# Banded attention followed by a gated MLP: dividing each pair's output instead of its attention weights, with one weight buffer fewer and a re-timed order

## The chip, the cores and the metric

The program runs on one core of one Trainium2 chip. The metric is the device time of one execution in microseconds (us), from a profiler-free run; a profiled execution has its own time as well. The engines are PE (TensorE, matrix products), DVE (VectorE), ACT (ScalarE), POOL (GpSimd) and SP (SyncE, which here only issues DMAs).

## The reference

Eight batches, eight heads, 576 tokens, head size 64, then a gated MLP on the 4608 joined tokens (512 to 1536 to 512), all in float32.

```python
scores = scale * np.matmul(q, k.transpose(0, 1, 3, 2))
thresh = np.max(scores, axis=-1, keepdims=True) - tau
scores = np.where(scores >= thresh, scores, -1000000000.0)
scores = scores - np.max(scores, axis=-1, keepdims=True)
attn = np.exp(scores)
attn = attn / (np.sum(attn, axis=-1, keepdims=True) + 1e-09)
attn_out = np.matmul(attn, v)
# x = attn_out as (tokens, 512)
out = (1 / (1 + np.exp(-(x @ w_gate))) * (x @ w_val)) @ w_out
```

Only scores within `tau` of a row's largest one keep a weight; the weights of a row are divided by their sum.

## The kernel before

**Attention.** The work is cut into 32 pairs (8 batches, 4 pairs of heads each; `b` and `hp` in the code, a name such as `0_3` is batch 0, pair 3). A pair has nine tiles of 128 query rows by 576 keys: four for each head and one, called `l`, that holds the 64 left-over rows of both heads. Per tile, in `tile_steps`: PE computes the scores `s` into PSUM (L638 in one plain float32 product for the first `NPS` pairs, L646 in split high and low halves for the others); DVE takes each row's maximum into `st` (L653); the threshold is made from it on POOL for early tiles and on DVE later (L662); ACT takes the exponential into `p` (L667); DVE zeroes what is under the threshold and adds up the row in the same instruction (L670, sums in `sm`). Then a group of two tiles (or the `l` tile) is normalised: DVE takes the reciprocal of the sums (L706) and POOL multiplies each tile of `p` by it (L708). PE transposes `p` (L719, and L732 for the last 64 keys), ACT copies the result out of PSUM into `pt` and `pl` (L677), and PE multiplies by the values (`av`, L755). ACT copies `av` into `xf`, the pair's output with 128 rows (2 heads of 64 columns) and 576 tokens. For batches 0 and 1 `xf` is split into halves for the MLP at once (`split_x`: ACT cast L765, POOL subtraction L767); for the others it goes to DRAM (`xp`, `xa`) and comes back later. The tokens of the left-over rows always go to DRAM.

**MLP.** Weights come from DRAM, are turned from raw words into high and low halves (`convert`: POOL L471, ACT L475, DVE L478 and L484, ACT L496, POOL L502), and are written back to DRAM. Batches 0, 1 and 2 are multiplied directly (`in_units` L815, `out_units` L858); the others in three double blocks with seven products instead of eight (`two_blocks`: `in_two` L1057, `out_two` L1122). The three direct blocks run on PE between the tiles of attention, from the moment that all four pairs of batch 0 are there; the double blocks follow.

**Order.** Nothing is ordered by hand. Every operation gets an engine, a cost and a key (its due time in tiles), and a list scheduler (`Plan.run`) with a model of buffers and DMA writes each engine's instruction order from them before the program runs; on the chip every engine then works strictly in that order and waits for semaphores. `SLOTS` gives the number of buffers of each kind, `LEAD` how many tiles ahead a pair's inputs are prepared, `CONV_IN` and `CONV_OUT` the due times of the weight conversions (first one, step), `AHEAD` how many units of matrix work ahead an MLP weight may be loaded, `SHIFT` by how many tiles everything from batch 1 on is due later, and `LAG` the delay that the scheduler assumes when an engine waits for another. MLP products have keys from 1e6 on, so that on PE they fill what attention leaves free. All DMAs but one are issued from SP's one queue, in order.

Of the kernel before, what the change touches and what calls it, by code (L numbers as in the profile page):

```python
# [43 lines left out]
class Plan:  # L44
# [10 lines left out]
    def buf(self, tag, shape, dtype, name, cls=None):  # L55
        return Buf(self, tag, shape, dtype, name, cls)
# [256 lines left out]
def kernel(  # L313
# [203 lines left out]
    class Visit:  # L517


        def __init__(self, b, hp, kind, first):  # L520
            self.b, self.hp, self.kind, self.first = b, hp, kind, first

            self.plain_s = 4 * b + hp < NPS
            self.of_tiles = {}
            self.name = f"{b}_{hp}{kind}"
            self.c0, self.c1 = {"": (0, SM), "a": (0, SM // 2), "b": (SM // 2, SM)}[kind]
            g0, g1 = [(0, (0, 1)), (1, (0, 1))], [(0, (2, 3)), (1, (2, 3))]
            left = [(None, (NJ,))]
            self.groups = {"": g0[:1] + left + g1[:1] + g0[1:] + g1[1:], "a": g0, "b": left + g1}[kind]
            self.with_left = kind != "a"  # L530
# [78 lines left out]
    def tile_steps(vis, g, i, key):  # L609

        h, qt = g.h, g.tiles[i]
        n = f"{g.name}{i}"


        s = buf("s", [P, 2, SM], F32, f"s{n}")
        kc = SL if i == 0 else 0
        sv = lambda: s.ap[:, :, :HALF]
        cols = None if h is None else slice(qt * P - vis.c0, (qt + 1) * P - vis.c0)
        if vis.plain_s:

            heads = [(0, SM, 0, SL), (1, SM, SL, P)] if h is None else [(h, qt * P, 0, P)]
            reads = [y for x, c0, *_ in heads for y in ((vis.q1, (x, int(c0 >= 2 * P))), vis.k1[x])]
        elif h is None:
            steps = [
                (lambda a=a: vis.q2.ap[:, a, vis.WM :], lambda c, z=z: vis.k2.ap[:, z, c])
                for a, z in ((0, 0), (0, 1), (1, 0))
            ]
            reads = [vis.q2, vis.k2]
        else:
            steps = [  # L630
                (lambda: vis.qd[h].ap[:, cols], lambda c, z=z: vis.kd[h].ap[:, z, c]) for z in range(2)
            ]
            reads = [vis.qd[h], vis.kd[h]]

        def plain_scores():
            for (x, c0, r0, r1), c in itertools.product(heads, range(2)):
                rows = slice(c * D, (c + 1) * D)
                nc.tensor.matmul(  # L638
                    s.ap[r0:r1, c, :HALF], vis.q1.ap[rows, x, c0 : c0 + r1 - r0],
                    vis.k1[x].ap[rows, kc : kc + HALF], start=True, stop=True, skip_group_check=True,  # L640
                )

        def scores():
            for m, (st, mv) in enumerate(steps):
                for c in range(2):
                    nc.tensor.matmul(  # L646
                        s.ap[:, c, :HALF], st(), mv(slice(kc + c * HALF, kc + (c + 1) * HALF)),
                        start=m == 0, stop=m == len(steps) - 1,
                    )
# [3 lines left out]
        op("DVE", 0.76, key, lambda: nc.vector.tensor_reduce(  # L653
            out=st.ap[:, 0:1], in_=sv(), axis=AX.XY, op=ALU.max, negate=True
        ), reads=[s], writes=[(st, 0)])
        thr = THR(vis.first)
        if thr == "ACT":
            op("ACT", 0.3, key, lambda: nc.scalar.activation(
                st.ap[:, 1:2], st.ap[:, 0:1], AF.Identity, bias=ntau_t[:, 0:1], scale=-1.0
            ), reads=[(st, 0)], writes=[(st, 1)])  # L660
        else:
            op(thr, 0.21 if thr == "DVE" else 0.3, key, lambda: {"DVE": nc.vector, "POOL": nc.gpsimd}[thr].tensor_scalar(  # L662
                out=st.ap[:, 1:2], in0=st.ap[:, 0:1], scalar1=-1.0, scalar2=ntau_t[:, 0:1],
                op0=ALU.mult, op1=ALU.add,
            ), reads=[(st, 0)], writes=[(st, 1)])
# [4 lines left out]
        op("DVE", 0.9, key, lambda: nc.vector.scalar_tensor_tensor(  # L670
            out=p(), in0=sv(), scalar=st.ap[:, 1:2], in1=p(),
            op0=ALU.is_ge, op1=ALU.mult, accum_out=g.sm.ap[:, i : i + 1],
        ), reads=[s, (st, 1)], writes=[(g.p, i), (g.sm, i)])
# [10 lines left out]
    class Group:  # L684


        def __init__(self, vis, h, tiles):
            self.vis, self.h, self.tiles = vis, h, tiles
            self.name = f"{vis.name}_{'l' if h is None else h}{tiles[0]}"
            n = self.n = len(tiles)  # L690
            c = "c" if h is None else ""
            self.p = buf("p" + c, [P, n * S], F32, f"p{self.name}")
            self.sm = buf("sm", [P, n], F32, f"sm{self.name}")

            self.z = h or 0
            if tiles not in vis.of_tiles:
                m = 1 if h is None else 2
                vis.of_tiles[tiles] = (
                    buf("pt" + c, [P, m, NJ, n * P], F32, f"pt{self.name}"),
                    buf("pl" + c, [P, m, P], F32, f"pl{self.name}"),  # L700
                )
            self.pt, self.pl = vis.of_tiles[tiles]

        def normalise(self, key):
            sm, p, n = self.sm, self.p, self.n
            op("DVE", 0.17, key, lambda: nc.vector.reciprocal(out=sm.ap, in_=sm.ap), writes=[sm])  # L706
            for i in range(n):
# [629 lines left out]
```

## Time and profile before

| | |
|---|---|
| time, three runs | 1343.53, 1349.85, 1351.82 us (median 1349.85) |
| profiled execution | 1344.67 us, of which the span of its instructions is 1342.9 us |
| granted TensorE clock | 0.999 |
| busy share of the span | PE 98%, weight loads 80%, DVE 71%, ACT 55%, POOL 48% |
| DMA | 311.55 MB in 138709 packets, mean 232 GB/s |

The span falls into three stretches. Until 96.79 us only attention and weight conversions run, since the first MLP product needs all of batch 0. From there to about 803 us PE alternates between attention and the direct MLP blocks. From 824.79 us on the double blocks run alone. A busy time is the union of the intervals in which an engine executed something; the idle time before an instruction is put down to what released it.

### The profile page before, as it was taken

How to read it: one execution, taken by the hardware profiler on the slowest of the kernel's cores; microseconds unless marked ns; L12 is line 12 of the kernel's file. 1: busy time of each engine (PE TensorE's matmuls, PEld its weight loads, DVE VectorE, ACT ScalarE, POOL GpSimd, SP SyncE). 2: the span in 40 equal slices, each digit the busy share in tenths (PEclk: the TensorE clock that was granted, in tenths of full speed). 3: DMA queues.
4: the chain of work that ended last, by engine and by line, in shares of the span. 5: the costliest groups of instructions: out<-in, count | busy, mean ns of one | idle time of the engine just before them, and what ended most of it. 6: DMA issues, size and time to landing. Idle time of an engine off the chain costs nothing.

```text
span 1342.9 us, 23617 instructions
## 1 busy us (share of the span) xinstructions
PE 1316.9 (98%) x8292; PEld 1078.1 (80%) x8292; DVE 952.0 (71%) x1918; ACT 732.9 (55%) x1349; POOL 639.6 (48%) x675
## 2 busy tenths in 40 slices
PE   7889999999999999999999999999999999999998
PEld 4568878888888888888888878888888888888887
DVE  7888777777777787777877853557955569554593
ACT  7787777767767677666767652213522235322242
POOL 7788968965867765767767641111001010001100
PEclk9999999999999999999999999999999999999999
DMA  8679889998878796897968848656685566756563
GB/s 302 178 230 340 273 249 295 280 265 214 269 207 263 226 276 178 239 288 239 260 209 239 253 147 321 203 184 207 208 294 190 194 198 209 244 180 205 185 220 119
DMA packets 138709, 311.55 MB, mean 232 GB/s; under 512 B 21856, under 2 KB 49760, under 8 KB 138592
## 3 DMA queue, kind: packets, MB, share of 16 engines
q1 hardware_dynamic: 138448, 310.04, 75.1%
q8 instruction: 67, 1.10, 0.3%
q14 instruction: 50, 0.41, 0.1%
q10 hardware_dynamic: 144, 0.00, 0.0%
HBM read 204.08 MB, written 54.53 MB: 193 GB/s over the span
## 4 chain that ended last, share of the span: by engine, by line
PE 88%; DMA 3%; POOL 2%; ACT 2%; DVE 1%; issue 1%; SPq 1%; POOLq 0%; DVEq 0%; ACTq 0%
PE m L815 14%; PE qb L1057 11%; PE av L755 10%; PE s L646 8%; PE tp L719 8%; PE qc L1057 7%; PE qa L1057 7%; PE o L858 6%; PE rb L1122 5%; PE rc L1122 4%; PE ra L1122 4%; PE s_l L646 2%; DMA wr<-in_moe_w_out_dram 1%; PE lk L732 1%; DMA wo<-wod 1%
## 5 line engine op out<-in xcount | busy, mean ns | idle before, releaser
L708 POOL TENSOR_SCALAR p<-p,zero_t,sm 128x576 f32<-128x576 f32 x256 | 216.3, 855 | 91.8 <-DVE sm L706 73.4
L653 DVE TENSOR_REDUCE st<-s 128x1 f32<-128x576 f32 x256 | 192.0, 753 | 82.1 <-PE s L646 75.5
L670 DVE SCALAR_TENSOR_TENSOR p<-s,st,p 128x576 f32<-128x576 f32 x256 | 205.6, 811 | 29.0 <-ACT p L667 20.9
L970 POOL TENSOR_TENSOR gA<-gA 128x512 f32<-128x512 f32 x18 | 24.1, 1340 | 422.7 <-DVE gA L1036 422.7
L667 ACT ACTIVATE p<-s,st 128x576 f32<-128x576 f32 x256 | 189.4, 748 | 48.5 <-DVE st L653 46.5
L677 ACT COPY pt<-tp 128x512 f32<-128x512 f32 x256 | 147.5, 587 | 55.8 <-PE tp L719 53.8
L646 PE MATMUL s<-kd,qd 128*128 128x288 f32 x896 | 161.3, 307 | 1.0 <-DVE p L670 0.7
L815 PE MATMUL m<-x,wi 128*128 128x512 f32 x576 | 161.1, 404 | 0.0
L719 PE MATMUL tp<-ident,p 128*128 128x128 f32 x1024 | 153.1, 276 | 8.0 <-POOL p L708 2.6
L719 PEld LDWEIGHTS tp<-ident,p 128*128 128x128 f32 x1024 | 118.9, 140 | 38.8 <-issue 9.3
L646 PEld LDWEIGHTS s<-kd,qd 128*128 128x128 f32 x896 | 132.7, 190 | 9.9 <-PE m L815 0.9
L755 PE MATMUL av<-pt,vs 128*64 128x256 f32 x1024 | 124.6, 385 | 0.8 <-ACT pt L677 0.7
L858 PE MATMUL o<-g,wo 128*128 128x512 f32 x432 | 117.8, 402 | 0.0
L815 PEld LDWEIGHTS m<-x,wi 128*128 128x128 f32 x576 | 99.3, 189 | 14.1 <-ACT pl L677 0.2
L1057 PE MATMUL qa<-xs_p,wa 128*128 128x512 f32 x432 | 109.6, 389 | 0.0
L994 DVE TENSOR_TENSOR qu<-qb,qp 128x512 f32<-128x512 f32 x72 | 49.8, 691 | 83.9 <-PE qb L1057 69.8
L755 PEld LDWEIGHTS av<-pt,vs 128*64 128x64 f32 x1024 | 67.8, 136 | 47.7 <-issue 10.3
L1057 PEld LDWEIGHTS qa<-xs_p,wa 128*128 128x128 f32 x432 | 81.1, 188 | 16.8
L858 PEld LDWEIGHTS o<-g,wo 128*128 128x128 f32 x432 | 75.3, 189 | 11.1 <-ACT pl L677 0.2
L815 PE MATMUL m<-x,ws 128*128 128x512 f32 x288 | 76.7, 406 | 1.2 <-ACT pl L677 0.8
L1032 ACT ACTIVATE gA<-qa 128x512 f32<-128x512 f32 x18 | 10.8, 598 | 103.3 <-PE qa L1057 103.3
L962 ACT CAST gs_p<-gA 128x512 fp32r<-128x512 f32 x54 | 32.4, 619 | 58.2 <-DVE gA L1036 25.1
(141 smaller groups left out, 2577.4 us busy)
## 6 DMA issues: line engine op xcount, KB each, us to landing
kd<-k SPq DMA_DIRECT2D x112, 320.0 KB, 5.8
wi<-wid SPq DMA_DIRECT2D x48, 512.0 KB, 6.9
wo<-wod SPq DMA_DIRECT2D x36, 512.0 KB, 7.0
wa<-wid SPq DMA_DIRECT2D x36, 512.0 KB, 4.3
ws<-sid SPq DMA_DIRECT2D x36, 512.0 KB, 4.9
wt<-sid SPq DMA_DIRECT2D x36, 512.0 KB, 4.8
wo_p<-sod SPq DMA_DIRECT2D x36, 512.0 KB, 4.9
qd<-q SPq DMA_DIRECT2D x112, 128.0 KB, 4.3
```

The source lines that it names most:

```text
L646: nc.tensor.matmul(s.ap[:, c, :HALF], st(), mv(slice(kc + c * HALF, kc + (c + 1) * HALF)), start=m == 0, stop=m == len(steps) - 1,)
L653: op("DVE", 0.76, key, lambda: nc.vector.tensor_reduce(out=st.ap[:, 0:1], in_=sv(), axis=AX.XY, op=ALU.max, negate=True), reads=[s], write ...
L667: op("ACT", 0.74, key, lambda: nc.scalar.activation(p(), sv(), AF.Exp, bias=st.ap[:, 0:1], scale=1.0), reads=[s, (st, 0)], writes=[(g.p, i)])
L670: op("DVE", 0.9, key, lambda: nc.vector.scalar_tensor_tensor(out=p(), in0=sv(), scalar=st.ap[:, 1:2], in1=p(), op0=ALU.is_ge, op1=ALU.mult ...
L677: return op("ACT", act(n), key, lambda: nc.scalar.copy(dst(), src.ap), reads=[src], writes=[part])
L708: op("POOL", 0.9, key, lambda i=i: nc.gpsimd.tensor_scalar(out=p.ap[:, i * S : (i + 1) * S], in0=p.ap[:, i * S : (i + 1) * S], scalar1=zer ...
L719: nc.tensor.matmul(tp.ap[:, c, :], self.p.ap[:, o + c * P : o + (c + 1) * P], ident, is_transpose=True, start=c == 0, stop=c == NJ - 1, sk ...
L755: nc.tensor.matmul(av.ap[h * D : (h + 1) * D, a:z], vis.vs.ap[:, j, h], m(h), start=i == 0, stop=i == len(ms) - 1, skip_group_check=True,)
L815: nc.tensor.matmul(m.ap, wv[:, a, c * P : (c + 1) * P], xs[c].ap[:, z, c0:c1], start=e == 0, stop=e == 11,)
L858: nc.tensor.matmul(acc.ap, wv[:, f, a], g[fg * ND + f].ap[:, z], start=(fg, f, a, z) == (0, 0, 0, 0), stop=(fg, f, a, z) == (NFG - 1, ND - ...
L1057: nc.tensor.matmul(acc.ap, wv[:, y, (2 * h + c) * P : (2 * h + c + 1) * P], xt[prod][c].get()[:, z], start=e == 0 and prod in FIRST, stop= ...
L1122: nc.tensor.matmul(acc.ap, w.ap[:, e, c, y], gt[prod][2 * g + c].get()[:, z], start=m == 0 and g == 0 and prod in FIRST, stop=m == 5 and g ...
```

## The change

For every pair but `0_3` (the last one of batch 0) the weights in `p` stay undivided: their reciprocal and the nine POOL multiplications go. In their place stands one step per pair, `late_normalise`. The nine sums of each row lie in one 128 x 32 tile (`sums`, three in rotation, filled with 1.0 at the start); DVE takes the reciprocals of nine columns and transposes the tile in blocks of 32 x 32 (`turned`); four DMAs write the nine rows of each block to a DRAM tensor `rd` (9 x 128); four DMAs read it back, each row broadcast to the 64 rows of its head, into `rb` (128 x 576); POOL multiplies `xf` by `rb`. Whatever reads `xf` now comes after that. `p` has three buffers instead of four, which makes room for `rb`. Plain scores are used for three pairs instead of four, and seven numbers of the scheduler change.

```diff
-    "p": 4, "pc": 1, "sm": 8, "st": 16, ... "xf": 2, "x": 6, "g": 12,
+    "p": 3, "pc": 1, "sm": 8, "st": 16, ... "xf": 2, "rb": 1, "x": 6, "g": 12,
-LEAD = 8
-CONV_IN, CONV_OUT = (36, 2), (56, 3)
+LEAD = 9
+CONV_IN, CONV_OUT = (36, 2.5), (56, 3)
-AHEAD = 4
+AHEAD = 5
-NPS = 4
+NPS = 3
-SHIFT = 35
+SHIFT = 50
-LAG = {"PE": 1.0, "DVE": 0.3, "ACT": 0.08, "POOL": 0.3, "SP": 0.08}
+LAG = {"PE": 0.8, "DVE": 0.2, "ACT": 0.3, "POOL": 0.3, "SP": 0.08}
+
+def LATE(b, hp):
+    return (b, hp) != (0, 3)
...
+    rows_of = [(lasting(f"sums{i}"), lasting(f"turned{i}")) for i in range(3)]
+    for sm, _ in rows_of:
+        nc.vector.memset(sm.t, 1.0)
...
-            op0=ALU.is_ge, op1=ALU.mult, accum_out=g.sm.ap[:, i : i + 1],
-        ), reads=[s, (st, 1)], writes=[(g.p, i), (g.sm, i)])
+            op0=ALU.is_ge, op1=ALU.mult, accum_out=g.sums(i),
+        ), reads=[s, (st, 1)], writes=[(g.p, i), g.parts[i]])
+
+    def late_normalise(vis, key):
+        n = 2 * NJ + 1
+        sm, rt, name = vis.sm, vis.rt, vis.name
+        op("DVE", 0.17, key, lambda: nc.vector.reciprocal(out=sm.ap[:, :n], in_=sm.ap[:, :n]), writes=[sm])
+        op("DVE", 0.2, key, lambda: nc.vector.transpose(out=rt.ap, in_=sm.ap), reads=[sm], writes=[rt])
+        rd = dram([n, P], f"rd{name}")
+        for c in range(P // 32):
+            rows = slice(32 * c, 32 * c + n)
+            op("SP", 0.1, key, lambda c=c, rows=rows: nc.sync.dma_start(
+                out=rd.t[:, 32 * c : 32 * c + 32], in_=rt.ap[rows]
+            ), reads=[rt], writes=[(rd, c)])
+        rb = buf("rb", [P, S], F32, f"rb{name}")
+        for h in range(2):
+            rows = slice(h * D, (h + 1) * D)
+            op("SP", 0.5, key, lambda h=h, rows=rows: nc.sync.dma_start(
+                out=rb.ap[rows, :SM],
+                in_=rd.t[h * NJ : (h + 1) * NJ].rearrange("t q -> (t q)").unsqueeze(0).to_broadcast([D, SM]),
+            ), reads=[rd], writes=[(rb, (h, 0))])
+            op("SP", 0.1, key, lambda h=h, rows=rows: nc.sync.dma_start(
+                out=rb.ap[rows, SM:], in_=rd.t[2 * NJ : n, h * SL : (h + 1) * SL].to_broadcast([D, SL])
+            ), reads=[rd], writes=[(rb, (h, 1))])
+        op("POOL", 1.5, key, lambda: nc.gpsimd.tensor_tensor(out=vis.xf.ap, in0=vis.xf.ap, in1=rb.ap, op=ALU.mult),
+           reads=[rb], writes=[vis.xf])
...
         def normalise(self, key):
+            if self.vis.late:
+                return
...
             if h == 1:
                 g.output(c, t - 1 + 0.3)
+        if vis.late:
+            late_normalise(vis, t)
```

Since the scheduler decides the order, the rows of the programs themselves show what moves. The first place is POOL's queue before the subtraction that completes `x_3`, the last input of the first MLP product. Before, eleven rows stand between the normalisation of pair `0_3`'s last group and `x_3`; these are the last seven of them and `x_3` (`ws`, `wa` are conversions, `k` is the split of a pair's keys, `p_0_00` belongs to batch 1):

```order
L662 TENSOR_SCALAR st_0_l_1188<-st_0_l_1188,ntau_t 128x1
L471 TENSOR_SCALAR wa_2_1241<-wr_2_1190,zero_t 128x512
L565 TENSOR_TENSOR k_1_1233<-kn_1_504,k_1_1233 128x640
L502 TENSOR_TENSOR ws_0_1250<-wa_0_881,ws_0_1250 128x512
L708 TENSOR_SCALAR p_0_00_1181<-p_0_00_1181,zero_t,sm_0_00_1210 128x576 x2
L471 TENSOR_SCALAR wa_0_1316<-wr_0_1246,zero_t 128x512
L502 TENSOR_TENSOR ws_1_1312<-wa_1_946,ws_1_1312 128x512
L767 TENSOR_TENSOR x_3_1327<-xf_3_1243,x_3_1327 128x512
```

Now, on the same engine from the same normalisation (L756, the pair that is still divided early) on:

```order
L756 TENSOR_SCALAR p_3_12_1190<-p_3_12_1190,zero_t,sm_3_12_1202 128x576 x2
L483 TENSOR_SCALAR wa_0_1281<-wr_0_1128,zero_t 128x512
L483 TENSOR_SCALAR wa_2_1288<-wr_2_1157,zero_t 128x512
L514 TENSOR_TENSOR ws_0_1286<-wa_0_857,ws_0_1286 128x512
L514 TENSOR_TENSOR ws_2_1382<-wa_2_915,ws_2_1382 128x4x128
L815 TENSOR_TENSOR x_3_1402<-xf_3_1304,x_3_1402 128x512
```

Four conversions are left between the two; the normalisation of batch 1's first tiles, a key split and the thresholds are gone from this stretch. The second place is PE's queue just before the first MLP product (`m_0_0_0`). Before (`tp`, `lk` are transposes, `s` scores, all of pair `1_0`):

```order
L755 MATMUL av_3_12_1271<-pl_3_l_1137,vs_3_570 64x64 x2
L719 MATMUL tp_0_000_1319<-ident,p_0_00_1181 128x128 x4
L719 MATMUL tp_0_001_1331<-ident,p_0_00_1181 128x128 x4
L646 MATMUL s_0_100_1340<-kd_0_1_839,qd_0_1_972 128x288 x4
L732 MATMUL lk_0_00_1355<-ident,p_0_00_1181 128x128
L815 MATMUL m_0_0_0_1373<-x_0_577,ws_0_465 128x512 x3
```

Now, from the same last value product of pair `0_3`:

```order
L803 MATMUL av_3_12_1349<-pl_3_l_1186,vs_3_567 64x64 x2
L661 MATMUL s_0_101_1387<-kd_0_1_1065,qd_0_1_1047 128x288 x4
L767 MATMUL tp_0_001_1397<-ident,p_0_00_1254 128x128 x4
L780 MATMUL lk_0_00_1405<-ident,p_0_00_1254 128x128
L767 MATMUL tp_0_l_1418<-ident,p_0_l_1296 128x128 x4
L780 MATMUL lk_0_l_1432<-ident,p_0_l_1296 128x128
L767 MATMUL tp_0_020_1441<-ident,p_0_02_1372 128x128 x4
L661 MATMUL s_0_120_1453<-kd_0_1_1065,qd_0_1_1047 128x288 x4
L767 MATMUL tp_0_021_1463<-ident,p_0_02_1372 128x128 x4
L780 MATMUL lk_0_02_1472<-ident,p_0_02_1372 128x128
L863 MATMUL m_0_0_0_1477<-x_0_604,ws_0_578 128x512 x3
```

Counted over the whole queue, PE has done two more score tiles and three more transposed tiles of pair `1_0` when the first MLP product comes. The third place is SP's queue at a late normalisation in the middle of the program (`sid` and `wi` are MLP weights on their way out and in, `qd` and `kd` the queries and keys of a coming pair):

```order
L841 DMA wi_3_0_4460<-wid_0_110 128x1024
L700 DMA rd_0_197<-turned_132 9x32 x4
L593 DMA qd_2_0_4573<-q_2_4567 64x512
L706 DMA rb_0_4576<-rd_0_197 64x512
L710 DMA rb_0_4576<-rd_0_197 64x64
L706 DMA rb_0_4576<-rd_0_197 64x512
L710 DMA rb_0_4576<-rd_0_197 64x64
L593 DMA qd_2_0_4573<-q_2_4567 64x512
L597 DMA kd_2_0_4607<-k_2_4541 64x2x640 x2
```

Eight DMAs are new there. The four reads of `rd` follow its four writes with one other DMA in between, and the inputs of the next pair stand behind them.

More of the change, by code (lines that the diff above doesn't have):

```diff
@@ L226 @@
     "kn": 1, "qn": 1, "vn": 1, "k2": 1, "q2": 1, "kd": 3, "qd": 3, "vs": 3,
-    "p": 4, "pc": 1, "sm": 8, "st": 16, "pt": 2, "pl": 2, "ptc": 1, "plc": 1, "xf": 2, "x": 6, "g": 12,
+    "p": 3, "pc": 1, "sm": 8, "st": 16, "pt": 2, "pl": 2, "ptc": 1, "plc": 1, "xf": 2, "rb": 1, "x": 6, "g": 12,
     "w": 9, "t2": 6,
 }
-LEAD = 8
-CONV_IN, CONV_OUT = (36, 2), (56, 3)
+LEAD = 9
+CONV_IN, CONV_OUT = (36, 2.5), (56, 3)
 EARLY = 16
-AHEAD = 4
+AHEAD = 5
 PAD = 64
-NPS = 4
+NPS = 3
 AV_COST = 0.0096
@@ L443, with lasting @@
     w_sb = {}
+    def lasting(name):
+        b = Buf(plan, None, [P, 32], F32, name)
+        b.t = cp.tile([P, 32], F32, tag=name, name=name)
+        return b
+    rows_of = [(lasting(f"sums{i}"), lasting(f"turned{i}")) for i in range(3)]
+    for sm, _ in rows_of:
+        nc.vector.memset(sm.t, 1.0)
     def convert(i, f, key):
@@ L523, in __init__ @@
             self.plain_s = 4 * b + hp < NPS
+            self.late = LATE(b, hp)
+            if self.late:
+                self.sm, self.rt = rows_of[(4 * b + hp) % len(rows_of)]
             self.of_tiles = {}
@@ L692, in __init__ @@
             self.p = buf("p" + c, [P, n * S], F32, f"p{self.name}")
-            self.sm = buf("sm", [P, n], F32, f"sm{self.name}")
+            if vis.late:
+                at = 2 * NJ if h is None else h * NJ + tiles[0]
+                self.sums, self.parts = (lambda i: vis.sm.ap[:, at + i : at + i + 1]), [(vis.sm, at + i) for i in range(n)]
+            else:
+                sm = self.sm = buf("sm", [P, n], F32, f"sm{self.name}")
+                self.sums, self.parts = (lambda i: sm.ap[:, i : i + 1]), [(sm, i) for i in range(n)]
             self.z = h or 0
@@ L1213, in attention @@
                 g.output(c, t - 1 + 0.3)
+        if vis.late:
+            late_normalise(vis, t)
         b, hp = vis.b, vis.hp
```

## Prediction

> **What bounds the kernel now.** I read the busy shares first, then busy time by stretch, then who waited for whom inside a stretch.
>
> ```profile
> PE 1316.9 (98%) x8292; PEld 1078.1 (80%) x8292; DVE 952.0 (71%) x1918; ACT 732.9 (55%) x1349; POOL 639.6 (48%) x675
> ...
> core 0: us, PE busy (x) PEld busy (x) DVE busy (x) ACT busy (x) POOL busy (x), PEclk, DMA share, GB/s
> 0.00:97.00 97.00, 80.62 (x648) 52.13 (x649) 78.58 (x169) 78.99 (x149) 75.43 (x115) 1.00 0.73 236
> 97.00:200.00 103.00, 100.11 (x636) 81.34 (x637) 82.15 (x170) 75.75 (x141) 83.21 (x86) 0.98 0.92 287
> 200.00:800.00 600.00, 597.14 (x4605) 498.78 (x4601) 457.59 (x1087) 412.90 (x776) 426.79 (x436) 1.00 0.84 243
> 800.00:1342.90 542.90, 539.03 (x2409) 445.87 (x2408) 333.66 (x495) 165.29 (x284) 54.21 (x40) 1.00 0.64 208
> ```
>
> PE is the bound: 26.0 us of 1342.9 are idle. 16.4 of the idle (97.00 - 80.62) lie before the first MLP product, 2.9 + 2.9 in the two stretches that follow, 3.9 at the end. No term of this change shortens PE's products by much, so all of the idle together, 1.9%, caps the gain. In the front, PE, DVE, ACT and POOL are each 78 to 83% busy: there the engines hand tiles to each other and no one is full.
>
> ```profile
> PE lk L732 <- ACT pt L677: 3.5, 5, 0.8
> PE s_l L638 <- DVE p L670: 2.0, 1, 2.0
> PE s L638 <- DVE p L670: 1.4, 2, 1.2
> ...
> DVE p L670 <- POOL st L662: 4.3, 6, 2.7
> DVE st L653 <- PE s L638: 3.6, 4, 2.0
> ...
> PE tp L719 <- POOL p L708: 2.2, 4, 0.9
> ```
>
> The first five rows are waits up to 97 us (in all, how many, the longest), the last one is PE's from 200 to 800 us. In the front DVE waits 4.3 us for a threshold that stands behind normalisations in POOL's queue, and PE then waits 3.4 for DVE. Later on PE waits for a normalisation itself for only 2.2 us in 600.
>
> **The change, part by part.** The removed work is large and mostly hidden.
>
> ```profile
> L708 POOL TENSOR_SCALAR p<-p,zero_t,sm 128x576 f32<-128x576 f32 x256 | 216.3, 855 | 91.8 <-DVE sm L706 73.4 <-PE s L646 9.2 <-PE av L755 4.0
> ...
> L565 POOL TENSOR_TENSOR k<-kn,k 128x640 fp32r<-128x640 f32 x2 | 3.1, 1559 | 0.3 <-PE av L755 0.3
> L767 POOL TENSOR_TENSOR x<-xf,x 128x512 fp32r<-128x512 f32 x4 | 5.1, 1270 | 0.3 <-ACT x L765 0.3
> L478 DVE SCALAR_TENSOR_TENSOR wb<-wb,wa 128x512 int32<-128x512 int32 x11 | 7.6, 691 | 3.4 <-ACT wb L475 3.4
> L706 DVE RECIPROCAL sm<-sm 128x2 f32<-128x2 f32 x17 | 2.8, 166 | 0.6
> L568 DVE SCALAR_TENSOR_TENSOR q<-qn,scale_t,q 128x640 fp32r<-128x640 f32 x2 | 2.2, 1114 | 0.0
> ```
>
> POOL loses 31 x 9 x 0.855 = 239 us and gains 31 products of 128x576, between the 1.27 of 512 columns and the 1.56 of 640, say 1.42: 44 us. It is busy 48% and not the bound, so of this only what waits for POOL counts.
>
> *Threshold.* Of the 4.3 us I take 3.3; 1.0 stays, as thresholds still stand behind conversions and the new product.
>
> *The last input of the MLP.*
>
> ```profile
> 80.97 0.17 DVE L706 RECIPROCAL sm<-sm 128x2 f32<-128x2 f32 x1
> ...
> 93.38 0.62 ACT L765 CAST x<-xf 128x512 fp32r<-128x512 f32 x1
> ...
> 91.07 1.63 POOL L708 TENSOR_SCALAR p<-p,zero_t,sm 128x576 f32<-128x576 f32 x2
> 92.68 1.41 POOL L471 TENSOR_SCALAR wa<-wr,zero_t 128x512 f32<-128x512 f32 x1
> 94.05 1.27 POOL L502 TENSOR_TENSOR ws<-wa,ws 128x512 fp32r<-128x512 f32 x1
> 95.29 1.26 POOL L767 TENSOR_TENSOR x<-xf,x 128x512 fp32r<-128x512 f32 x1
> ...
> 96.79 0.50 PE L815 MATMUL m<-x,ws 128*128 128x512 f32 x1 [0.75 <-ACT pl L677]
> ```
>
> The cast of `x_3` ended at 94.00, its subtraction began at 95.29 because POOL was full, and the first MLP product followed at 96.79. With four conversions left in that place POOL is free: 1.3 us.
>
> *DVE ahead of pair 0_3's last tile* (by the two programs' rows): one conversion more, two steps of 0.69; one more query split, 1.11; 7 reciprocals for 19, 12 x 0.166 = 2.0 saved; three block transposes, which the trace does not have, between the reciprocal's 0.17 and a query split's 1.11, taken at 0.2, as 32 columns are nearer to the reciprocal's 2 than to 640. Sum +1.1 us, with 1.0 to 3.8 by the ends.
>
> *PE work brought forward.*
>
> ```profile
> 108.62 0.69 PE L646 MATMUL s<-kd,qd 128*128 128x288 f32 x4
> 109.15 1.08 PE L815 MATMUL m<-x,ws 128*128 128x512 f32 x4
> ...
> 106.04 0.60 PE L719 MATMUL tp<-ident,p 128*128 128x128 f32 x4
> 106.39 0.71 PE L815 MATMUL m<-x,ws 128*128 128x512 f32 x2
> ```
>
> From start to next start a score tile takes 0.53 and a transposed tile 0.35. Two and three more of them before the first MLP product are 2.1 us of PE work done in idle time.
>
> *Later.* The 2.2 us that PE waited for `p` go; what was queued next on PE was already there, so nothing replaces them.
>
> *Pair 0_3 in split scores, `LEAD`, `CONV_IN`, three `p` buffers.* Counted at 0: PE executes four products of 288 columns per tile either way, the splits were prepared for other pairs beside attention before, and a `p` tile is held for less time. If that cover goes, a tile waits for one normalisation, 1.63 us, some three times in the front.
>
> *The way round through DRAM.* The first pair of rows is of the front, the second from 97 to 800 us.
>
> ```profile
> L1228 SPq DMA_DIRECT2D xp<-xf x3: 561/567/628, 36.4 to 76.0; - x3
> DMA to landing us min/median/max: 2.5/2.9/3.4
> ...
> L1228 SPq DMA_DIRECT2D xp<-xf x28: 522/611/1399, 98.6 to 782.8; - x28
> DMA to landing us min/median/max: 2.1/4.7/9.5
> ...
> SPq L578 <- ACT q L563: 126.0, 21, 10.8
> ...
> kd<-k SPq DMA_DIRECT2D x112, 320.0 KB, 5.8
> ...
> qd<-q SPq DMA_DIRECT2D x112, 128.0 KB, 4.3
> ...
> 802.90 22.05 PE L858 MATMUL o<-g,wo 128*128 128x512 f32 x96
> ...
> 810.58 1.29 POOL L970 TENSOR_TENSOR xb<-xb,xb 128x512 f32<-128x512 f32 x1 [15.59 <-DMA xb<-xp]
> ```
>
> The nearest DMA is the small one of 32 KB: 0.6 us to issue, landing after 2.9 us in the front and 4.7 (2.1 to 9.5) later. From the last sum to `rb`: 0.4 on DVE, four issues 2.4 of which the last lands 2.9 after its start, again 1.8 + 2.9: 9.8 us in the front, 13.4 later. SP waits in order, so behind the reads of `rd` stand the next pair's `qd` and `kd`; behind POOL's product stand thresholds and conversions. In the front, `xf` is complete some 12 us after the last sum (pair `0_3`: reciprocal at 80.97, cast of `x_3` at 93.38); without a reciprocal and two products of 0.82 between them it will be some 10, so `rb` is about in time. Later, a pair lasts (802.90 - 96.79) / 28 = 25.2 us. Eight DMAs per pair are those of the two rows for `kd` and `qd`; with `kn`, `qn`, `vs`, one or two from `xf` and some five of MLP weights SP issues an estimated 18, at 0.6 each 11 us. It gets 8 x 0.6 + 4.7 = 9.5 more: 20.5 of 25.2. It fits, and its 126 us of waiting for query splits (4.5 per pair) show the room. New waits on PE: between 0 and 28 us (rival below), taken at 1.5, near 0, as weights are asked for five units ahead. [...]
>
> *The end of attention.* After the last value product PE has 96 MLP products, 22.05 us, and the first double block's inputs are used 7.7 us after it. The new product delays `xf` by 1.42 or somewhat more, and by the new program's rows 70 products remain, 16.1 us: 9.1 of 16.1, hidden; a delay of over 7 us would show.
>
> The sum: -3.3 - 1.3 + 1.1 - 2.1 - 2.2 + 1.5 = -6.3 us, against the profiled 1344.67: 1338.4. That execution lay 5.2 under the median of the three runs; on their basis it is 1343.6. I say 1343.
>
> **The rivals.**
> *The front closes* (0.2). Every hand-over in it gets shorter by a reciprocal and a normalisation, and PE loses all waits but the start's: 16.4 less the 5 us before the first tile can be there, and 2.9 + 2.2 later: 1344.67 - 16.5 = 1328.2, 1333 on the runs' basis. For it: the waits of DVE and PE above feed each other. Against it: DVE's work ahead of the last tile does not fall.
> *Nothing* (0.2). ACT's casts of `x_0` to `x_2` and POOL's thresholds stand behind `rb`; three waits of 2 us cancel the -6.3: 1350.
> *SP becomes the bound, slower* (0.1). It decides from 25.2 us of SP per pair on: with the landing at its longest 9.5 in place of 4.7, SP has 25.3. Each us over costs 28. At 1 us over, 1338.4 + 28 = 1366, 1371 on the runs' basis. For it: the DMA share of 0.92 and 0.84 in these stretches and the order of the rows. Against it: SP's waits.
> *The clock* (0.05).
>
> ```profile
> 97.60:101.00 3.40, 3.40 (x10) 2.62 (x9) 3.29 (x8) 1.72 (x4) 0.49 (x3) 0.50 1.01 243
> ```
>
> Once, after gaps of 0.76 and 0.75, 3.4 us ran at a granted clock of 0.50, a loss of 1.7. A front with a different pattern has none or several: -1.7, or +1.7 for each; two more, 1347. [...]
>
> **How the numbers follow.** Forecast 0.45, its own range 1337 to 1350 (the DVE ends, the threshold from 0 to 4.3, run to run). The range must take in the front's closing at 1333 less a few us, and a part of the slower side: 1328 to 1360, which leaves out the SP case and the tails. A measurement of this kernel tells about 1% (13.5 us) from no change. Faster by over 1% (under 1336.4): most of the first rival, 0.15, and a little of the forecast: 0.19. Slower (over 1363.3): the SP case and a tail, 0.11. Within: 0.70.
>
> **What the changed profile would show.** The first MLP product at about 93 us, with PE idle before it down from 16.4 to about 11. The wait of DVE for `st` on POOL at 1 us; no wait of PE for a normalised `p` after 200 us. POOL's busy time near 445. SP's waits for `rd` near 28 x 4, without new waits of PE for `kd`, `wi` or `wo`. Such waits of over 5 us, casts of `x` that wait over 2 us for POOL, or a first product after 95 us, would make it wrong.

## The result, and the profile after

The changed kernel takes 1363.87 us (median of 6 runs) and the kernel before 1348.76 us (6 runs on the same chip). The ratio is 1.0119, 95% interval 1.0076 to 1.0162: **1.2% slower**, 16 us by the ratio and 15.1 by the medians. The forecast was 1343 us with a range to 1360. The profiled execution took 1364.27 us, 19.6 more than that of before: PE's idle time rose from 26.0 to 39.4 us, its busy time by 6.2.

The busy shares, the four stretches of before, and two groups of POOL, changed kernel:

```profile
PE 1323.1 (97%) x8290; PEld 1089.2 (80%) x8290; DVE 942.9 (69%) x1848; ACT 726.4 (53%) x1339; POOL 452.9 (33%) x419
...
0.00:97.00 97.00, 80.46 (x644) 55.59 (x645) 79.24 (x167) 77.16 (x145) 55.07 (x84) 0.98 0.83 261
97.00:200.00 103.00, 100.14 (x671) 82.07 (x670) 85.48 (x175) 79.97 (x153) 65.63 (x57) 0.97 0.98 304
200.00:800.00 600.00, 584.40 (x4426) 489.93 (x4426) 428.62 (x968) 388.19 (x731) 270.03 (x232) 0.99 0.85 249
...
L713 POOL TENSOR_TENSOR xf<-xf,rb 128x576 f32<-128x576 f32 x31 | 44.9, 1448 | 92.0 <-DMA rb<-rd 62.3 <-ACT p L682 11.5 <-DMA qd<-q 9.7
L957 POOL TENSOR_TENSOR s<-wi 128x512 f32<-128x512 f32 x24 | 33.0, 1376 | 106.8 <-DMA wi<-wid 101.9 <-DMA rd<-turned 4.4 <-POOL k L580 0.4
```

POOL is as light as forecast (445 us forecast, 452.9 measured; the product 1.45 us). But from 200 to 800 us PE is idle for 600 - 584.40 = 15.6 us, where it was 2.9 before. L957 is the first addition of the weight sums that the double blocks need (L909 before). POOL waited 20.8 us for its load in the kernel before, and waits 101.9 now; ACT's cast of the sums (L920 before, L968 now) waited 0.4 us for POOL, and now 18.6. Kernel before, 97 to 800 us:

```profile
POOL s L909 <- DMA wi<-wid: 20.8, 9, 4.3
...
ACT s L920 <- POOL s L909: 0.4, 1, 0.4
```

Waits between 97 and 800 us in the changed kernel (total, times, longest), for PE, ACT, POOL and SP's queue:

```profile
PE lk L780 <- ACT pt L718: 4.5, 1, 4.5
PE s L661 <- DVE p L685: 3.7, 4, 3.1
PE tp_l L767 <- ACT pt L718: 3.6, 3, 1.9
PE tp L767 <- ACT xf L718: 3.1, 2, 2.6
...
ACT s L968 <- POOL s L957: 18.6, 10, 3.6
...
POOL s L957 <- DMA wi<-wid: 101.9, 20, 9.6
POOL xf L713 <- DMA rb<-rd: 48.1, 11, 14.8
...
SPq L706 <- DMA rd<-turned: 50.0, 25, 4.5
...
SPq L593 <- ACT q L578: 7.9, 4, 3.2
```

PE's loss is not spread out: five stalls of over 1 us between 200 and 800 us (at 354.58, 390.07, 423.94, 518.90 and 683.47 us) make 13.5 of the 15.6. The chain of waits of the changed kernel shows the third of them from its start at SP:

```profile
404.47 0.62 SPq L597
...
405.14 2.01 SPq L841
...
407.26 1.03 SPq L1267
...
408.34 0.65 SPq L1278
...
409.72 6.12 DMA wi<-wid
...
415.97 1.29 POOL s L957
...
422.80 0.61 ACT s L968
423.41 0.49 ACT pt L718
...
423.94 0.33 PE tp_l L767
```

The load of a weight for the sums goes out behind a row of other issues and lands 6.1 us after its own; POOL, whose next work this is, is already waiting; ACT's cast of the sum (L968) waits for POOL; the tile copy `pt` stands behind that cast in ACT's fixed order; PE waits 1.95 us for the copy. The stall at 390.07 has this form too. The load takes no longer than it did: from its issue to its last semaphore update in the trace, `wi` took 6.9 us in the kernel before and 6.8 now (medians of 48). What moved is when it is issued and when POOL asks for it.

The largest stall (4.54 us at 518.90) has the same form with ACT's cast of an `x` that came back from DRAM (`xa`, landing 6.27 us after its issue) in place of the sum. Here SP's queue shows how a wait for `rd` reaches a load; SP's wait from 490 to 512 us and two of its issues:

```profile
SPq L706 <- DMA rd<-turned: 4.1, 1, 4.1
...
496.05 0.48 SPq L706 DMA_DIRECT2D rb<-rd  x1
...
511.45 0.43 SPq L1301 DMA_DIRECT2D xa<-xa  x1
```

SP stands 4.1 us for `rd`, then issues eighteen DMAs with hardly a gap, and only then comes the load of `x`. The stalls at 354.58 and 683.47 us start at the round trip itself (`rd` landing 4.99 and 5.67 us after its issue, `rb` 2.79 and 2.68, then POOL's product, a sum, ACT's cast, ACT's exponential).

PE also runs at half clock more often: twice before its first MLP product, and behind the stalls of 4.54 and 3.08 us. These are the stretches of the changed kernel (granted clock is the third number from the end):

```profile
44.20:47.60 3.40, 3.40 (x18) 1.92 (x18) 2.99 (x8) 2.01 (x3) 0.84 (x3) 0.50 0.77 311
102.20:109.00 6.80, 6.34 (x21) 4.82 (x20) 5.98 (x13) 4.74 (x9) 3.05 (x3) 0.50 1.05 321
518.60:522.00 3.40, 3.09 (x9) 2.42 (x10) 0.59 (x1) 3.40 (x8) 3.07 (x3) 0.50 0.09 23
682.50:689.30 6.80, 5.83 (x20) 5.05 (x21) 4.04 (x10) 3.60 (x8) 3.25 (x3) 0.50 1.03 282
```

Together 20.4 us at 0.50 against 3.4 before. Half of the difference, 8.5 us, is an estimate of what that added to the profiled execution. The two stretches behind the stalls alone cost 5.1 us by the same estimate.

### The profile page after: what moved, and what is told of

Read it like the earlier page. It is cut to its first block, busy times and chain, and to the rows that moved or that the text cites. A ratio compares the mean times of both kernels' runs of the same rounds, so it can differ in the third digit from the quotient of the medians.

```text
span 1362.5 us, 23334 instructions
## 1 busy us (share of the span) xinstructions
PE 1323.1 (97%) x8290; PEld 1089.2 (80%) x8290; DVE 942.9 (69%) x1848; ACT 726.4 (53%) x1339; POOL 452.9 (33%) x419
## 4 chain that ended last, share of the span: by engine, by line
PE 80%; DMA 9%; SPq 4%; ACT 2%; DVE 2%; issue 2%; POOL 2%; POOLq 0%; ACTq 0%; DVEq 0%
PE m L863 11%; PE qb L1105 11%; PE av L803 8%; PE qa L1105 7%; PE qc L1105 7%; PE s L661 7%; PE o L906 6%; PE tp L767 6%; PE rb L1170 5%; PE rc L1170 4%; PE ra L1170 4%; DMA rd<-turned 1%; PE s_l L661 1%; DMA xp<-xf 1%; DMA kd<-k 1%
## 5 line engine op out<-in xcount | busy, mean ns | idle before, releaser
L661 PE MATMUL s<-kd,qd 128*128 128x288 f32 x928 | 169.4, 306 | 5.1 <-DVE p L685 4.3
L863 PE MATMUL m<-x,wi 128*128 128x512 f32 x576 | 165.5, 409 | 1.4 <-ACT pt L718 1.4
L767 PE MATMUL tp<-ident,p 128*128 128x128 f32 x1024 | 157.4, 278 | 7.0 <-ACT xf L718 3.8
L661 PEld LDWEIGHTS s<-kd,qd 128*128 128x128 f32 x928 | 141.6, 190 | 20.0 <-DVE p L685 5.7
L767 PEld LDWEIGHTS tp<-ident,p 128*128 128x128 f32 x1024 | 122.1, 142 | 31.3 <-issue 6.4
L863 PE MATMUL m<-x,ws 128*128 128x512 f32 x288 | 80.4, 412 | 0.6 <-ACT pt L718 0.5
L713 POOL TENSOR_TENSOR xf<-xf,rb 128x576 f32<-128x576 f32 x31 | 44.9, 1448 | 92.0 <-DMA rb<-rd 62.3
L957 POOL TENSOR_TENSOR s<-wi 128x512 f32<-128x512 f32 x24 | 33.0, 1376 | 106.8 <-DMA wi<-wid 101.9
```

The source lines that it names most:

```text
L661: nc.tensor.matmul(s.ap[:, c, :HALF], st(), mv(slice(kc + c * HALF, kc + (c + 1) * HALF)), start=m == 0, stop=m == len(steps) - 1,)
L767: nc.tensor.matmul(tp.ap[:, c, :], self.p.ap[:, o + c * P : o + (c + 1) * P], ident, is_transpose=True, start=c == 0, stop=c == NJ - 1, sk ...
L863: nc.tensor.matmul(m.ap, wv[:, a, c * P : (c + 1) * P], xs[c].ap[:, z, c0:c1], start=e == 0, stop=e == 11,)
```

## The experiments

Each group of runs has its own runs of the kernel before (medians 1348.9 to 1350.3 us), so ratios are compared; "us" behind a ratio is the ratio's distance from 1 times 1350. On this scale the changed kernel is +16.1. PE's idle time is that from 200 to 800 us in the profile (2.9 before, 15.6 after).

**Is it the round trip?** The eight DMAs are planned, but not issued; the order stays. The four reads are edited as the writes are.

```diff
-            op("SP", 0.1, key, lambda c=c, rows=rows: nc.sync.dma_start(
-                out=rd.t[:, 32 * c : 32 * c + 32], in_=rt.ap[rows]
-            ), reads=[rt], writes=[(rd, c)])
+            op("SP", 0.1, key, lambda: None, reads=[rt], writes=[(rd, c)])
...
-        op("POOL", 1.5, key, lambda: nc.gpsimd.tensor_tensor(out=vis.xf.ap, in0=vis.xf.ap, in1=rb.ap, op=ALU.mult),
+        op("POOL", 1.5, key, lambda: nc.gpsimd.tensor_tensor(out=vis.xf.ap, in0=vis.xf.ap, in1=ones, op=ALU.mult),
```

> The changed kernel with the same order on every engine, but the eight DMAs per pair that carry the reciprocal sums (`rd`, `rb`) are not issued, and POOL multiplies `xf` by a constant tile of ones; the transport of the sums is left out. Theory 1 (POOL, freed of normalisations, runs the weight sums as soon as their loads land, the loads land later than planned, and ACT's casts of the sums, in ACT's fixed order, hold up tile copies and exponentials that PE waits for): PE's stalls at 354 and 683 us, which the chain of waits leads back to `rb`, go; those at 390, 424 and 519, led back to late weight loads, stay at least in part: 1352 to 1359 us. Theory 2 (the round trip itself: eight more DMAs per pair on SP's queue and the waits for `rd` make every load late): all five go and the time is that of before or better, 1342 to 1349. Theory 3 (the new numbers of the order, not the round trip): no change, 1362 to 1366.

Measured 1338.55 us, ratio 0.9925 (0.9909 to 0.9942), -10 us. All stalls are gone:

```profile
200.00:800.00 600.00, 598.75 (x4586) 503.56 (x4586) 444.37 (x1004) 402.05 (x752) 275.85 (x235) 1.00 0.81 241
```

So the transport costs 26 us, and what is left of the change gains 10. Theory 1 in its first form falls: the stalls that led to late weight loads went too. POOL is as light here, and still waits 54.4 us for the loads of the sums between 97 and 800 us, but no stall of PE follows.

**What of the round trip?** Three kernels keep all eight DMAs and the order, and take waits away by changing what is read: POOL's product reads ones (`e5`), the fills of `rb` read a constant tensor in DRAM (`e6`), or both (`e7`). The first edit is that of `e5`, the second, made in the narrow reads too, that of `e6`. All three leave the sums out of the result. The product that reads ones takes 1.17 us in place of 1.45.

```diff
-in0=vis.xf.ap, in1=rb.ap, op=ALU.mult
+in0=vis.xf.ap, in1=ones[:, :1].to_broadcast([P, S]), op=ALU.mult
```

```diff
-in_=rd.t[h * NJ : (h + 1) * NJ].rearrange("t q -> (t q)").unsqueeze(0).to_broadcast([D, SM]),
+in_=fixed[h * NJ : (h + 1) * NJ].rearrange("t q -> (t q)").unsqueeze(0).to_broadcast([D, SM]),
```

> The changed kernel with the same order; all eight DMAs per pair are issued and SP still waits for the landing of `rd`, but POOL's product reads a constant of ones and does not wait for `rb` (the sums reach no output). If the loss of 25 us that leaving out the transport showed comes from POOL's wait for `rb` and what stands behind it on POOL and ACT: near 1339 to 1344 us. If it comes from SP (its issue time and its wait for `rd` hold up the loads behind) or from the bytes: 1357 to 1366.

> The changed kernel with the same order and the same eight DMAs per pair, but the four that fill `rb` read a constant tensor in DRAM instead of `rd`, so SP waits for no landing of `rd` (about 50 us of waiting between 97 and 800 us); POOL still waits for `rb`. The sums reach no output. If SP's wait in order is the cause: most of the 25 us go, 1339 to 1347. If it is SP's issue time (8 x 0.6 us per pair) or the traffic: 1356 to 1366. If it is POOL's wait for `rb`: in between, since `rb` lands some 5 us earlier.

> Both of the edits before together: the eight DMAs per pair are issued and move their bytes, but nobody waits for them. What is left above the run without transport (1339 us) is the price of SP's issue time and of the traffic alone: 1339 to 1343 if the waits are the cause, 1356 to 1366 if issue time or traffic is.

In a fourth kernel, on top of `e7`, each read fills one row of `rb`:

```diff
-out=rb.ap[rows, :SM],
-in_=fixed[h * NJ : (h + 1) * NJ].rearrange("t q -> (t q)").unsqueeze(0).to_broadcast([D, SM]),
+out=rb.ap[h * D : h * D + 1, :SM],
+in_=fixed[h * NJ : (h + 1) * NJ].rearrange("t q -> (t q)").unsqueeze(0),
```

> The kernel of the run in which all eight DMAs are issued and nobody waits for them (1348 us), but each of the four reads fills one row of `rb` in place of 64: SP issues as many, 10 MB fewer are moved. Without any transport it was 1339. If the traffic is what those 9 us are: 1338 to 1342. If SP's issue time is: 1346 to 1350.

| run | SP waits for `rd` | POOL waits for `rb` | bytes of `rb` | ratio (interval) | us | PE idle |
|---|---|---|---|---|---|---|
| changed kernel | yes | yes | all | 1.0119 (1.0076 to 1.0162) | +16.1 | 15.6 |
| `e5` | yes | no | all | 1.0090 (1.0056 to 1.0125) | +12.2 | 12.3 |
| `e6` | no | yes | all | 0.9993 (0.9972 to 1.0013) | -0.9 | 7.3 |
| `e7` | no | no | all | 0.9993 (0.9971 to 1.0015) | -0.9 | 6.6 |
| `e9` | no | no | 1/64 | 0.9929 (0.9910 to 0.9948) | -9.6 | 3.0 |
| `e1` | none issued | | | 0.9925 (0.9909 to 0.9942) | -10.1 | 1.3 |

The last column from the rows of 200 to 800 us, of `e5`, `e6`, `e7` and `e9` in this order:

```profile
200.00:800.00 600.00, 587.75 (x4479) 494.30 (x4478) 432.44 (x982) 393.10 (x738) 264.64 (x234) 0.99 0.85 250
```
```profile
200.00:800.00 600.00, 592.73 (x4529) 498.38 (x4527) 439.96 (x997) 398.43 (x749) 274.48 (x237) 1.00 0.87 252
```
```profile
200.00:800.00 600.00, 593.38 (x4522) 499.20 (x4521) 440.79 (x994) 397.82 (x747) 267.25 (x236) 1.00 0.87 253
```
```profile
200.00:800.00 600.00, 597.04 (x4567) 502.24 (x4567) 443.51 (x1004) 401.43 (x752) 270.87 (x237) 1.00 0.83 242
```

`e5` and `e7` differ in what the reads of `rb` read, and so in SP's wait for the landing of `rd` (50.0 us in `e5`, none in `e7`): 13 us by the ratios, give or take 6. The other source is not the reason: the wide reads landed 3.0 us after their issue from `rd` in `e5` and 3.4 from the constant in `e7` (medians). The largest stall goes with this wait; PE's waits for a tile copy before `lk`, in `e5` and in `e7`, from 97 to 800 us:

```profile
PE lk L784 <- ACT pt L722: 4.7, 2, 4.4
```
```profile
PE lk L784 <- ACT pt L722: 0.8, 1, 0.8
```

`e6` and `e7` differ in POOL's wait for `rb` (37.9 us in `e6`, none in `e7`): nothing by the ratios, as long as `rb` is filled early. With SP's wait in place, POOL's adds about 4 (changed kernel against `e5`), which is not clear of noise, as the intervals overlap. `e7` and `e9` differ by 8.7 us, give or take 4, through the width of the reads; that is not the bytes alone, as the issue of such a read got shorter too, from `e7` to `e9` (ns, shortest, median, longest):

```profile
L710 SPq DMA_DIRECT2D rb<-fixed x54: 444/594/1163, 124.1 to 786.0; - x54
```
```profile
L710 SPq DMA_DIRECT2D rb<-fixed x55: 214/253/1376, 120.5 to 799.5; - x55
```

Bytes and issue time of these reads are not told apart. The four writes of `rd` and the four one-row reads that `e9` keeps cost nothing that shows (0.5 us against `e1`, within the intervals).

**Is it ACT's cast of the sums?** The casts of L968 keep their length and wait for nothing.

```diff
-            op("ACT", act(512), key, lambda t=t: nc.scalar.copy(full(t, 0), f32(full(t, 1))), writes=[t])
+            op("ACT", act(512), key, lambda: nc.scalar.copy(free, f32(free)), writes=[t])
```

> The changed kernel with the same order, but ACT's casts of the weight sums (L968) read and write a tile that is always ready, so they keep their 0.6 us and wait for nothing; the rounded upper part of the sums is left out. Theory 1: the stalls of PE that run through that cast (354, 390, 424, 553, 683 us) go with the half clock behind them, the one of 519 us (a cast of x that waits for its load) stays: 1348 to 1353 us. Theory 2 (loads late for PE by themselves): the stalls come back through another instruction, 1358 to 1366. Theory 3: 1362 to 1366.

1361.6 us, ratio 1.0097 (1.0080 to 1.0115). It gains at most a few us: the stalls at 354, 390, 424 and 683 us are gone, but that at 519 has grown from 4.54 to 6.30, and there are new ones of 1.64 at 440, 2.21 at 480 and 2.42 at 799 us. So the cast carries stalls, but is not their cause: loads that are late reach PE by another instruction.

**Is it the numbers?** `e3` and `e16` are the kernel before with the new numbers (with three and four tiles of `p`), `e4` the changed kernel with the old ones, `e17` the same without transport, `e20` late normalisation in the first three pairs alone, with the old numbers. Of the diff of the change, `e3` and `e16` take the numbers from `LEAD` to `LAG` (`e3` also `"p": 3`), the other three undo them (and keep `"p": 3`). `e20` has in addition:

```diff
-    return (b, hp) != (0, 3)
+    return b == 0 and hp != 3
```

> The kernel before with only the new numbers: three tiles of `p`, LEAD 9, CONV_IN 2.5, AHEAD 5, NPS 3, SHIFT 50 and the new LAG; normalisation as before. Theories 1 and 2: the numbers alone cost little, 1343 to 1354 us. Theory 3: the loss is there without the late normalisation, 1358 to 1368.

> The changed kernel with the old numbers (LEAD 8, CONV_IN 2, AHEAD 4, NPS 4, SHIFT 35, the old LAG), keeping the late normalisation, three tiles of `p` and one of `rb`. Theories 1 and 2: casts of sums on ACT still wait for POOL and loads, the stalls come at other places, 1354 to 1372 us. Theory 3: the loss goes, 1342 to 1350.

> The kernel before with the new numbers LEAD, CONV_IN, AHEAD, NPS, SHIFT and LAG, but its four tiles of `p`; normalisation as before. With three tiles it took 1360.6 us. If the missing tile is what cost 11 us there (normalised tiles are held longer): 1346 to 1353. If the other numbers did: 1357 to 1364.

> The changed kernel with the old numbers and without the transport (constant ones in place of `rb`; the sums are left out). With the new numbers it took 1339 us. If the gain of 11 us against the kernel before is that of the freed POOL: 1336 to 1342. If the new numbers are needed for it, as the changed kernel with old numbers at 1380 suggests: 1345 to 1356.

> The changed kernel with the old numbers, three tiles of `p`, and the late normalisation only in the first three pairs of batch 0; all other pairs normalise their tiles as the kernel before does. If the loss is made between 200 and 800 us by 28 round trips: 1343 to 1356, near the kernel before. If the round trip or the missing tile of `p` already costs in the front: 1357 to 1368.

| normalisation | old numbers | new numbers |
|---|---|---|
| of `p`, as before | 0 | +8.9 (`e3`, 1.0034 to 1.0099), +10.1 with four `p` (`e16`, 1.0057 to 1.0094) |
| late, with transport | +30.4 (`e4`, 1.0193 to 1.0257) | +16.1 |
| late, no transport | -6.1 (`e17`, 0.9940 to 0.9970) | -10.1 |
| late in three pairs of the front | +4.3 (`e20`, 1.0017 to 1.0047) | |

The numbers are worth nothing by themselves: 9 to 10 us lost with the old normalisation (the missing tile of `p` is not why), 4 gained without transport, 14 gained with it. With the transport they take off some of its loss. With both sets of numbers the transport is what costs: 36.5 us with the old ones, 26.2 with the new. `e20` shows no gain of the late normalisation in the front, with its transport there and three tiles of `p`.

**Ways round the wait.** All keep the whole computation. `e8` lets the planner place the reads and the product later; `e14` and `e15` keep the order and let four or eight other DMAs of SP go ahead of the reads; `e11` issues the reads from POOL, `e18` from ACT with the landing planned in; `e12` has three DMAs per pair in place of eight, `e13` the same with the reads on POOL.

The edits of `e8`, of `e14` (`LATER` holds the four reads, `FLUSH` POOL's products; `e15` has 8), of `e18` and of `e12`; `e11` and `e13` only put `nc.gpsimd` for `nc.sync` at the reads, of the changed kernel and of `e12`.

```diff
-            ), reads=[rd], writes=[(rb, (h, 0))])
+            ), reads=[rd], writes=[(rb, (h, 0))], lag=3.0)
...
-           reads=[rb], writes=[vis.xf])
+           reads=[rb], writes=[vis.xf], lag=2.5)
```

```diff
         for o in order:
+            if o.emit in LATER:
+                held.append(o)
+                left = 4
+                continue
+            if held and (not left or o.emit in FLUSH):
+                for x in held:
+                    x.emit()
+                held = []
             o.emit()
+            left -= o.eng == "SP" and left > 0
```

```diff
-            op("SP", 0.5, key, lambda h=h, rows=rows: nc.sync.dma_start(
+            op("ACT", 0.55, key, lambda h=h, rows=rows: nc.scalar.dma_start(
...
-            ), reads=[rd], writes=[(rb, (h, 0))])
+            ), reads=[rd], writes=[(rb, (h, 0))], lag=3.0)
```

```diff
+out=rd.t.rearrange("r (c q) -> c r q", c=P // 32), in_=rt.ap
...
+out=rb.ap[:, :SM],
+in_=rd.t[: 2 * NJ].rearrange("(h t) q -> h (t q)", h=2).unsqueeze(1).to_broadcast([2, D, SM]),
...
+out=rb.ap[:, SM:],
+in_=rd.t[2 * NJ].rearrange("(h q) -> h q", h=2).unsqueeze(1).to_broadcast([2, D, SL]),
```

> The whole changed kernel, with one thing told to the planner that sets the order: the reads of `rd` may be placed only 3.0 us later than it took the writes to land, and POOL's product 2.5 us later than it took `rb` to land (as measured, a landing takes about 5 us, where the planner counts 2.5). If SP's wait in order or POOL's wait for `rb` is the cause, other DMAs and weight sums move ahead of them: 1340 to 1352 us. If issue time or traffic is the cause: no change within the noise of a new order, 1357 to 1368.

1.0170 (1.0145 to 1.0196). SP's wait for `rd` is out of the list, the time is not better; it is another order on every engine, so it settles nothing.

> The whole changed kernel; every engine's order is kept but SP's, where the four reads of `rd` into `rb` go out behind the next four other DMAs (or right ahead of POOL's product, if that comes first). If SP's wait in order costs the 15 us by holding up the loads behind it: 1347 to 1354 us. If the loss is not in that wait but in how early `rb` is there: 1362 to 1370, as POOL now waits longer.

> As the run with four DMAs let ahead, but with eight. By SP's wait: within 3 us of the run with four, as the wait is gone by then. If POOL's wait for `rb` costs something once it grows by some 3 us per pair: 3 to 10 us more than with four.

`e14` 1.0519 (1.0479 to 1.0560), +70 us; `e15` 1.0896 (1.0872 to 1.0919), +121 us. In this order the wait cannot be passed on by letting other DMAs go first. POOL's and SP's waits in `e15`:

```profile
POOL xf L727 <- DMA rb<-rd: 173.2, 19, 22.3
...
SPq L1283 <- POOL xf L727: 27.1, 11, 4.6
SPq L1287 <- POOL xf L727: 12.7, 4, 6.8
SPq L1294 <- POOL xf L727: 11.3, 3, 5.5
```

POOL waits 173 us for `rb`, with the weight sums and key splits behind it; and SP, freed at the reads, now stops for POOL's product, at the writes of `xf` (L1283 to L1294), which are ahead of the next loads. POOL's wait was free in `e6` because `rb` came early, not because nothing depends on it.

> The whole changed kernel in the same order, but the four reads of `rd` into `rb` are issued by POOL's queue at the place where SP issued them, so POOL, not SP, waits for the landing of `rd`. If SP's wait in order costs 15 us and POOL's waits cost nothing: 1343 to 1350. If a wait of this kind costs as much on POOL, because weight sums and splits stand behind it: 1355 to 1368.

> The whole changed kernel, with the four reads of `rd` issued by ACT and planned 3.0 us after the planner's landing of `rd` and POOL's product 2.5 us after that, so that neither SP nor (by the plan) ACT or POOL waits long. SP keeps four of the eight issues. If SP's wait is the main loss and ACT, 53% busy, has room for 4 x 0.55 us per pair: 1345 to 1356. If ACT's own in-order waits for `rd` hold up tile copies: 1365 to 1400.

`e11` 1.0209 (1.0185 to 1.0234), `e18` 1.0631 (1.0606 to 1.0656). In `e18`, the rows of ACT, POOL and SP:

```profile
ACT pt L718 <- DMA rb<-rd: 16.5, 4, 5.6
...
POOL xf L713 <- DMA rb<-rd: 84.2, 13, 16.3
...
SPq L700 <- DVE turned L696: 63.2, 21, 8.8
```

POOL waits longer, and SP now waits 63 us for the transposed sums at the writes, where it waited 13.8 in the changed kernel. Whichever in-order queue took the wait, others stood behind it. Why `e11` lost, with shorter waits for weight loads than the changed kernel, is not settled; its stalls are many and small.

> The whole changed kernel in the same order, with three DMAs per pair in place of eight, all on SP: one write of `rd` (all 128 rows of `turned`, 128 bytes each) and two reads, each for both heads. SP saves 5 issues per pair and still waits for `rd`. If issue time is part of the loss: 1353 to 1360; if only the wait and the traffic are: 1361 to 1366.

> Both edits: one write of `rd` on SP, two reads issued by POOL. If SP's wait and SP's issue time are the whole loss, this keeps the forecast gain: 1338 to 1345 us, under the kernel before. If traffic is the other 9 us: 1346 to 1350.

`e12` 1.0836 (1.0812 to 1.0861), +113 us; `e13` 1.2384 (1.2357 to 1.2410), +322 us. No expectation had this. The chain of waits of `e12`:

```profile
350.38 9.04 DMA rb<-rd
...
359.57 1.41 POOL xf L714
360.99 0.69 POOL s L958
...
362.22 0.61 ACT s L969
362.84 0.49 ACT pt L719
363.37 0.33 PE lk L781
```

POOL's product, a sum, ACT's cast and the tile copy carry the late `rb` to PE. The piece of 9.04 us is the narrow read, which was issued last. From each issue to the last update of its semaphore in the trace, medians from 97 to 800 us:

| | changed kernel | `e12` |
|---|---|---|
| write of `rd` | 5.2 us | 6.7 |
| wide read of `rb` | 3.2, 128 KB each | 8.8, 256 KB |
| narrow read of `rb` | 2.8, 16 KB each | 9.8, 32 KB |
| load of `kd` | 5.4 | 8.3 |
| load of `qd` | 4.6 | 7.8 |

The 32 KB of the narrow read need longer than 256 KB did, and the loads of `kd` and `qd` land later too. So fewer DMAs were no test of issue time. The merged read has 2 outermost (heads) where each of the old ones has 64 rows, and in the traces each old read ends with 16 updates of its semaphore, each merged one with a single update soon after its issue and two at the end. That the shape is what made it slower is the author's reading; no run changes the shape alone.

## Why the prediction was wrong, point by point

- **New waits, 1.5 us: the step that failed.** The transport costs 26 us (`e1` against the changed kernel). The prediction put it: "It fits, and its 126 us of waiting for query splits (4.5 per pair) show the room. New waits on PE: ... near 0, as weights are asked for five units ahead." The size of the round trip was about right: a landing of `rd` took 5.2 us in the median of 108 writes, 2.6 to 8.8 (4.7 forecast), and SP waited only 50 us for it (28 x 4 forecast). What was wrong is the test. Room on average was there: SP's waits from 97 to 800 us sum to 333 us before and to 221 after, 50 of them for `rd`, so SP never became the bound. But each wait delayed the loads behind it at that moment (4.1 us ahead of the load of `x` at 511.45), and PE did not stop for MLP products' weights, which are asked for ahead: it stopped behind the weights for the sums and the `x` from DRAM. Their readers on POOL and ACT stand in the same in-order queues as the tile work. The prediction named the next pair's `qd` and `kd`, thresholds and conversions as what stands behind, and not these two, though POOL's wait for the weights of the sums was in the profile before. Of the 26 us, 13 go with SP's wait, 9 with the width of the reads (bytes or issue time, not told apart), and the remaining 4 are within the noise.
- **Rival "SP becomes the bound" (0.1, 1371 us).** Its mechanism was half right: SP's queue is the place. That its time was near is luck, as its condition (25.2 us of SP per pair) was not met and was not needed.
- **Rival "nothing"** named thresholds and casts of `x` behind `rb`. It was ACT's casts of `x` from DRAM and of sums.
- **The front, -3.3 - 1.3 + 1.1 - 2.1: mis-sized, not there.** The front up to the first MLP product, changed kernel and `e1`:

```profile
0.00:104.27 104.27, 84.97 (x667) 58.55 (x667) 86.30 (x180) 83.81 (x158) 59.63 (x88) 0.97 0.85 263
```
```profile
0.00:100.39 100.39, 83.01 (x668) 57.34 (x668) 86.37 (x181) 83.37 (x158) 59.90 (x88) 0.98 0.84 265
```

  That product starts at 104.27 us (forecast 93) with PE idle for 19.3 us (forecast 11, before 16.4). Without transport it is 100.39 and 17.4. Some 20 PE products more precede it, as forecast, but they are not done in idle time: PE is busy for 4.5 us more, about the 2.1 of these products and, an estimate, 2.7 by half clock. POOL was free for the subtraction of `x_3`, as forecast, but that ends at 98.94, later than before (96.55), and the product comes 5.3 us behind it, after tile work that the new order puts first. DVE's wait for a threshold fell to 1.8 us (before 4.3, forecast 1.0), but PE's waits for tiles stayed; why they did is not settled. `e20` has no gain either.
- **PE's waits for a normalised `p`, -2.2: right.** None is left, and in `e1` PE's idle time from 200 to 800 us falls from 2.9 to 1.3, that from 97 to 200 from 2.9 to 1.2.
- **The sum without transport** was -7.8 (-6.3 less the 1.5); `e1` measured -10.1. The total agrees, but partly by other terms: of the 7.7 us between the two profiles' spans (1342.9 and 1335.2) 3.4 are PE's idle time and 4.3 PE's busy time, which no term had.
- **The numbers of the order at 0:** wrong in both directions, +9 or +10 with the old normalisation and -14 beside the transport. Which of them does it was not tried.
- **The clock (0.05):** the rival named up to two more windows; there was six times the time at half clock (20.4 us for 3.4), in windows of 3.4 or 6.8 us at 0.50. What opens one is not shown: the late windows open at stalls of 4.5 and 3.1 us, the early ones behind gaps of 1.7 and 0.9 us at most, and behind the stall of 2.6 us at 390.07 there is none.

## What to carry to other kernels

The average room of an in-order DMA queue did not price a wait in it: list the loads that stand behind it, who reads each, and what stands behind that reader on its engine; here 25 waits, 50 us in all and 4.5 at most, cost 13 us. With the normalisations gone from POOL, its weight sums came up before their loads had landed, and it waited for them longer than the 20.8 us of before. This was free without the transport (54.4 us of POOL's waiting, no stall); with it (101.9 us) ACT came to wait behind POOL, and PE behind ACT. A wait that was moved to another in-order engine was not removed (2.1% slower than before from POOL, 6.3 from ACT, where the changed kernel was 1.2), and the merged reads took longer than those they replaced (8.8 and 9.8 us for 3.2 and 2.8), and the loads behind them too (`kd` 8.3 us for 5.4); try one read of the new shape first.

## What the runs showed of the hardware

A broadcast read of 128 rows by 2 KB with the heads as outermost dimension landed 8.8 us after its issue and one of 128 rows by 256 bytes behind it after 9.8 (`e12`); reads of 64 rows landed after 3.2 and 2.8 (changed kernel; all medians). The updates of their semaphores at the end are 2 for the merged reads, 16 for those of 64 rows and 9 for the writes of 9 rows.

Issued from POOL's queue in the merged shape (`e13`), the reads made the kernel 322 us slower; between 97 and 800 us POOL was idle for 201 us at the narrow one with nothing that the profile shows to wait for:

```profile
POOL rb L710 <- issue: 201.2, 17, 17.8
```

The issue of a wide read of 64 rows took SP 0.59 us (`e7`), that of one row 0.25 us (`e9`). The block transposition of 128 x 32, not in the trace of before, took 0.21 us, as taken.
